# Splitting the last fc2 output group of a DiT block into 192, 128 and 64 columns, with the last two finished by VectorE

## The chip, the cores and the metric

The kernel runs on one core of a Trainium2 chip. Times are device microseconds (us) of one execution; most quotes are medians of several executions. The profile's span of the same execution is about 1.7 to 1.85 us shorter than its time. The engines are named as the profile names them: PE (TensorE matmuls), PEld (its weight loads), DVE (VectorE), ACT (ScalarE), POOL (GpSimd), SP (SyncE, which issues 70 of the 90 DMAs in the trace of the kernel before). A letter q behind an engine means its sequencer.

## The reference, cut to what matters

```python
B, N, D = (2, 256, 1152);  F = 4 * D
...                                        # adaLN, attention, projection give x, h2, gate_m
m = _gelu(h2 @ w_fc1) @ w_fc2              # fc1: [512, 4608], fc2: [512, 1152]
return x + gate_m * m
```

Only the last two lines are touched. In the kernel, fc2 writes 512 rows (4 tiles of 128) by 1152 columns (3 panels of 384); every output group sums over KF = 36 blocks of 128.

## The kernel before

```python
P = 128; PW = 384; KF = 36; NPD = 3; NT = 4
...
    groups = []
    for n in range(NPD):
        for t in range(NT):
            if n == NPD - 1 and t == NT - 1:
                groups.append((n, t, n * PW, 2 * P))                  # 256 columns
                groups.append((n, t, n * PW + 2 * P, PW - 2 * P))     # 128 columns
            else:
                groups.append((n, t, n * PW, PW))
    for gi, (n, t, c0, cw) in enumerate(groups):
        b = t // TPB
        last = gi == len(groups) - 1
        pacc = acc_tile([P, cw], "pacc")
        for kk in range(KF):
            j, r = divmod(n * KF + kk, 27)
            nc.tensor.matmul(pacc[:], gT[:, kk, t * P:(t + 1) * P],
                w_f2[j][:, r, c0 - n * PW:c0 - n * PW + cw],
                start=(kk == 0), stop=(kk == KF - 1))
        tmp = work.tile([P, cw], FP32, name="tmp", tag="tmp", bufs=3)
        nc.vector.tensor_tensor(tmp[:], pacc[:], gate_m[:, b, c0:c0 + cw], op=ALU.mult)
        o_sb = work.tile([P, cw], BF16, name="o_sb", tag="o_sb", bufs=3)
        (nc.vector if last else nc.gpsimd).tensor_tensor(
            o_sb[:], tmp[:], x1[:, t, c0:c0 + cw], op=ALU.add)
        nc.sync.dma_start(out_v[:, b, t % TPB, c0:c0 + cw], o_sb[:])
```

Each group ends in a VectorE multiply out of PSUM, an add (GpSimd, but VectorE for the last group), and an output DMA from SyncE.

## Time and profile before

| quantity | before |
|---|---|
| time, median of the first 3 executions | 242.99 us (242.89 to 243.03) |
| span of the profiled execution | 241.3 us |
| PE busy | 98% of the span |
| start of fc2 (first matmul of L806) to the end | 73.55 us |
| end of the last matmul to the end | 3.10 us |

The last two rows are read from the records of the trace. From the page of the kernel before, here are the busy times of the engines (part 1) and the shares of the chain that ended last (part 4).

```profile
PE 236.3 (98%) x1698; PEld 144.6 (60%) x1698; DVE 91.6 (38%) x194; ACT 60.1 (25%) x122; POOL 28.3 (12%) x47
...
PE 95%; DMA 2%; DVE 1%; SPq 0%; issue 0%; DVEq 0%
```

The kernel is bound by PE. So there are two ways to make it shorter: fewer PE nanoseconds, or a shorter tail behind the last matmul. The next fence is the chain of the kernel before, in order of time, in the window from 224 us on; columns are start in us, length in us, and what it was.

```profile
223.94 14.24 PE pacc L806 x123
238.18 0.03 issue
238.21 0.02 DVEq L812
238.23 0.04 issue
238.27 0.30 DVE tmp L812
238.57 0.02 issue
238.60 0.29 DVE o_sb L814
```

After PE come 0.3 us of multiply and 0.3 us of add on 128 columns; then the output DMA. The costs of the pieces stand in the groups by form, window from 165 us on (line, engine, operation, shapes, count; busy us and mean ns of one; idle time before).

```profile
L806 PE MATMUL pacc<-w_f,gT 128*128 128x384 bf16 x396 | 64.5, 326 | 0.0
L806 PE MATMUL pacc<-w_f,gT 128*128 128x256 bf16 x36 | 4.1, 273 | 0.0
L806 PE MATMUL pacc<-w_f,gT 128*128 128x128 bf16 x36 | 2.2, 219 | 0.0
...
L812 DVE TENSOR_TENSOR tmp<-pacc,gate 128x256 f32<-128x256 f32 x1 | 0.4, 425 | 3.4 <-PE pacc L806 3.4
L812 DVE TENSOR_TENSOR tmp<-pacc,gate 128x128 f32<-128x128 f32 x1 | 0.3, 291 | 1.6 <-PE pacc L806 1.6
L814 DVE TENSOR_TENSOR o_sb<-tmp,x 128x128 bf16<-128x128 f32 x1 | 0.3, 291 | 0.0
```

A matmul's mean ns (326 at 384 columns) is its latency, not its spacing: they overlap. The spacing (start to start, in the trace) is 162.5 ns at 384 columns, 109.2 at 256 and 55.8 at 128. That 2-column matmuls with a new 128x128 weight each can follow one another much faster shows in the timeline of PE at 22 us (start us, length us, engine, line, what, count): nine in 0.37 us, of which 0.163 us is one latency, so some 26 ns each (start to start the records have 28 ns once and 25 seven times).

```profile
22.21 0.37 PE L250 MATMUL pm<-sT,w_scale_a 128*128 128x2 bf16 x9
```

Here are the waits of SyncE in the window 236 to 242 us of the kernel before (who waited for whom: us in total, times, longest), and then, from the instructions of the line that carries the end of the program (L856), SyncE's semaphore checks that fall between the moment the last DMA is seen and the next instruction of SyncE's program end, a drain at 240.44 (window 240.36 to 240.42 us).

```profile
...
SPq L817 <- DVE o_sb L814: 1.0, 1, 1.0
...
SPq L856 <- DMA out_dram<-o_sb: 0.6, 1, 0.6
```

```profile
L856 SPq EVENT_SEMAPHORE  x1: 28/28/28, 240.4 to 240.4; - x1
```

SyncE waited 0.6 us for the last output DMA, and after it had come there was one check record left: the one that waited.

### The profile page before, as it was taken

What the parts mean: (1) busy time and instruction counts of PE and PEld (TensorE: products, weight loads), DVE (VectorE), ACT (ScalarE), POOL (GpSimd) and SP (SyncE); (2) the same over time, 40 slices, a digit from 0 to 9 for tenths busy, and PEclk for the clock granted to TensorE, in tenths of its full rate; (3) what the DMA queues carried; (4) which work ended last, traced back from release to release, by engine and by line L of the source; (5) the groups of instructions that cost most, each with busy time, mean ns of one, the idle gap of its engine ahead of it and who ended that gap; (6) DMA issues with size and microseconds to landing.
All of it is one profiled execution on the core that took longest, in us unless ns stands there. A gap on an engine that the chain in (4) does not pass through costs nothing.

```text
span 241.3 us, 3993 instructions
## 1 busy us (share of the span) xinstructions
PE 236.3 (98%) x1698; PEld 144.6 (60%) x1698; DVE 91.6 (38%) x194; ACT 60.1 (25%) x122; POOL 28.3 (12%) x47
## 2 busy tenths in 40 slices
PE   8899999999999999999999999999999999999994
PEld 5675444466667566888844444444666656666674
DVE  4842442319325678930002999950000000000001
ACT  6732322307215032770423333222000000000000
POOL 2300000001400324100000000001121111111111
PEclk9999999999999999999999999999999999999999
DMA  6999999998599994739999999999300000000000
GB/s 196 324 317 311 376 367 391 389 393 249 99 315 397 387 311 81 196 62 364 390 392 392 339 326 284 285 326 275 98 16 16 20 16 16 19 18 18 26 25 16
DMA packets 48925, 53.30 MB, mean 221 GB/s; under 512 B 9731, under 2 KB 36619, under 8 KB 48907
## 3 DMA queue, kind: packets, MB, share of 16 engines
q1 hardware_dynamic: 41312, 50.14, 62.6%
q10 hardware_dynamic: 7083, 1.72, 4.9%
q0 software_dynamic: 512, 1.19, 2.2%
q8 instruction: 13, 0.21, 0.4%
q14 instruction: 5, 0.04, 0.1%
HBM read 50.15 MB, written 1.19 MB: 213 GB/s over the span
## 4 chain that ended last, share of the span: by engine, by line
PE 95%; DMA 2%; DVE 1%; SPq 0%; issue 0%; DVEq 0%
PE pacc L806 29%; PE pacc L750 29%; PE pacc L697 7%; PE pacc L603 7%; PE pq L525 7%; PE pk L282 5%; PE pk L311 2%; DMA x_sb<-in_x_dram 2%; PE pa L644 2%; PE ps_s L560 2%; PE pn L420 2%; PE pt L267 1%; PE pm L250 1%; DVE stats L195 1%; PE pg L502 0%; SPq L88 0%
## 5 line engine op out<-in xcount | busy, mean ns | idle before, releaser
L750 PE MATMUL pacc<-hT,w_f 128*128 128x256 bf16 (+1 forms) x432 | 70.5, 326 | 0.0
L806 PE MATMUL pacc<-w_f,gT 128*128 128x384 bf16 (+2 forms) x468 | 70.5, 314 | 0.0
L806 PEld LDWEIGHTS <-gT 128*128 128x128 bf16 x468 | 44.4, 98 | 26.2
L750 PEld LDWEIGHTS <-w_f 128*128 128x128 bf16 x432 | 42.2, 98 | 27.6
L812 DVE TENSOR_TENSOR tmp<-pacc,gate 128x384 f32<-128x384 f32 (+2 forms) x13 | 6.9, 527 | 65.6 <-PE pacc L806 57.3
L782 ACT ACTIVATE gT<-pacc 128x512 bf16<-128x512 f32 x24 | 14.3, 597 | 32.7 <-PE pacc L750 32.7
L473 DVE SCALAR_TENSOR_TENSOR part<-w_gate_m,s,part 128x1152 f32<-128x1152 bf16 x16 | 21.4, 1414 | 0.0
L814 POOL TENSOR_TENSOR o_sb<-tmp,x 128x384 bf16<-128x384 f32 (+1 forms) x12 | 11.6, 971 | 53.9 <-DVE tmp L812 53.9
L697 PE MATMUL pacc<-w_o,big 128*128 128x384 bf16 x108 | 17.9, 326 | 0.0
L525 PE MATMUL pq<-hT,w_q 128*128 128x512 bf16 x81 | 17.8, 379 | 0.0
L603 PE MATMUL pacc<-w_v,hT 128*128 128x384 bf16 x108 | 17.7, 326 | 0.0
L603 PEld LDWEIGHTS <-hT 128*128 128x128 bf16 x108 | 10.5, 98 | 7.1 <-issue 0.3
L697 PEld LDWEIGHTS <-big 128*128 128x128 bf16 x108 | 10.4, 98 | 7.2 <-issue 0.4
L525 PEld LDWEIGHTS <-w_q 128*128 128x128 bf16 x81 | 7.9, 98 | 9.4
L282 PE MATMUL pk<-big,w_k 128*128 128x256 bf16 (+1 forms) x72 | 13.2, 325 | 0.0
L703 POOL TENSOR_TENSOR x<-tmp,x_sb 128x384 f32<-128x384 f32 x8 | 7.3, 911 | 26.3 <-DVE tmp L702 26.3
L471 DVE TENSOR_SCALAR part<-w_gate_m,s 128x1152 f32<-128x1152 bf16 x2 | 1.6, 818 | 22.2 <-DMA w_gate_m<-in_w_mod_dram 22.2
L495 POOL DMA_DIRECT2D gates_dram<-nat_v x2 | 1.1, 534 | 67.7 <-DVE nat_v L493 67.7
L282 PEld LDWEIGHTS <-w_k 128*128 128x128 bf16 x72 | 6.8, 97 | 3.5 <-issue 0.2
L771 ACT ACTIVATE gT<-pacc 128x512 bf16<-128x512 f32 x12 | 6.5, 597 | 9.1 <-PE pacc L750 9.1
L516 POOL DMA_DIRECT2D gates_dram<-nat x4 | 2.4, 596 | 49.8 <-DVE nat L513 48.4
L175 PE MATMUL pwarm<-zeros 128*128 128x256 f32 x18 | 6.7, 540 | 1.2 <-DVE eps_t L95 1.2
(106 smaller groups left out, 164.4 us busy)
## 6 DMA issues: line engine op xcount, KB each, us to landing
w_f<-in_w_fc_dram SPq DMA_DIRECT2D x12, 864.0 KB, 14.2
w_f<-in_w_fc_dram SPq DMA_DIRECT2D x3, 1728.0 KB, 10.1
w_f<-in_w_fc_dram SPq DMA_DIRECT2D x2, 2592.0 KB, 17.2
w_gate_a<-in_w_mod_dram SPq DMA_DIRECT2D x3, 864.0 KB, 14.4
w_v<-in_wqkv_dram SPq DMA_DIRECT2D x3, 864.0 KB, 15.4
w_o<-in_wo_dram SPq DMA_DIRECT2D x3, 864.0 KB, 14.7
w_shift_m<-in_w_mod_dram SPq DMA_DIRECT2D x3, 864.0 KB, 9.5
w_scale_m<-in_w_mod_dram SPq DMA_DIRECT2D x3, 864.0 KB, 15.8
```

Source lines behind the costliest of these rows:

```text
L175: nc.tensor.matmul(dst[:, 0:T // 2], zeros32[:, 0:P], zeros32, start=True, stop=True)
L282: nc.tensor.matmul(pk[m][:, c0:c1], w_k[:, k, m * P:(m + 1) * P], hT0[:, k, c0:c1], start=(k == 0 and c0 == 0), stop=(k == KD - 1), skip_g ...
L473: nc.vector.scalar_tensor_tensor(part[:, b, :], wg[:, k, :], s32[:, k, b:b + 1], part[:, b, :], op0=ALU.mult, op1=ALU.add,)
L525: nc.tensor.matmul(pq[m][:], w_q[:, k, m * P:(m + 1) * P], hT[:, k, :], start=(k == 0), stop=(k == KD - 1), skip_group_check=True,)
L603: nc.tensor.matmul(pacc[:], hT[:, k, t * P:(t + 1) * P], w_v[:, k, pnl * PW:(pnl + 1) * PW], start=(k == 0), stop=(k == KD - 1),)
L697: nc.tensor.matmul(pacc[:], aT[:, k, t * P:(t + 1) * P], w_o[:, k, c0:c1], start=(k == 0), stop=(k == KD - 1),)
L703: (nc.gpsimd if pool_add else nc.vector).tensor_tensor(x1[:, t, c0:c1], tmp[:], x_sb[:, t, c0:c1], op=ALU.add)
L750: nc.tensor.matmul(dst, w_f1[m // KD][:, k, ml * P:(ml + 1) * P], hT[:, k, c0:c1], start=start, stop=(k == KD - 1), **kw,)
L782: nc.scalar.activation(gT[:, m, :], pacc[:], ACT.Gelu_apprx_tanh)
L806: nc.tensor.matmul(pacc[:], gT[:, kk, t * P:(t + 1) * P], w_f2[j][:, r, c0 - n * PW:c0 - n * PW + cw], start=(kk == 0), stop=(kk == KF - 1),)
L812: nc.vector.tensor_tensor(tmp[:], pacc[:], gate_m[:, b, c0:c0 + cw], op=ALU.mult)
L814: (nc.vector if last else nc.gpsimd).tensor_tensor(o_sb[:], tmp[:], x1[:, t, c0:c0 + cw], op=ALU.add)
```

## The change

The intent is a shorter tail: only 64 columns instead of 128 are left to multiply, add and store after the last matmul. To keep GpSimd's slower add out of the way (on 128 columns it took 0.45 us in run e7 below, against 0.29 on VectorE), the second to last piece is finished by VectorE too.

```diff
             if n == NPD - 1 and t == NT - 1:
-                groups.append((n, t, n * PW, 2 * P))
-                groups.append((n, t, n * PW + 2 * P, PW - 2 * P))
+                for c0, c1 in ((0, PW // 2), (PW // 2, PW - 64), (PW - 64, PW)):
+                    groups.append((n, t, n * PW + c0, c1 - c0))
...
-        last = gi == len(groups) - 1
+        last = gi >= len(groups) - 2
```

## The prediction

> What bounds the kernel now. The page gives PE 98% busy at a granted clock of 1.0 throughout, and the chain that ended last is 95% PE. The last stage (fc2, 468 matmuls, 29% of the span) is PE back to back: the table of groups shows no PE idle. The chain of waits ends with PE until 238.18 us, VectorE multiply 238.27 (0.29 us), VectorE add 238.60 (0.29), the last output DMA issued at 238.91 (0.33 to issue, landing about 1.1 us after its issue began), then about 1.2 us of program end; span 241.3. So two things matter: the PE time of the last 384 columns, and the 3.1 us tail behind the last matmul.
>
> What the change does. Two accumulation groups (256, 128 columns) become three (192, 128, 64): 36 more weight loads and matmuls, same columns. The new last group leaves 64 instead of 128 columns to finish; the 128-column group is finished by VectorE too and is now second to last. Nothing else moves; one more output DMA on SyncE's queue.
>
> PE cost. In the trace the spacing of matmuls in fc2 is 162.5 ns at 384 columns, 109.2 at 256, 55.8 at 128: a line of 2.5 ns plus 0.417 ns per column. Whether 64 columns follow that line depends on the weight load, which has less to hide under. Each LDWEIGHTS record lasts 98 ns, but they overlap: the 2-column matmuls of the scale section, each with its own 128x128 weights, run at 25 ns spacing in this trace. [...] So I estimate 29.2 ns at 64 columns and 82.5 at 192. PE for the 384 columns: before 36 x (109.2 + 55.8) = 5.94 us; after 36 x (82.5 + 55.8 + 29.2) = 6.03 us. Cost: +0.09 us, all on the chain.
>
> Tail gain. VectorE multiplies took 0.558, 0.425, 0.291 us at 384, 256, 128 columns, 1.05 ns per column, so 0.224 at 64; the add (0.291 at 128) should shrink alike. Two of them: -0.13 us. The last DMA writes 128-byte instead of 256-byte pieces; its packets took 28 ns at 512 bytes, 18 at 256, about 8 per engine: at most -0.04 us; the fixed part stays. Total tail: -0.13 to -0.18.
>
> No new wait: the 128-column group needs about 0.65 us of VectorE after its last matmul while the 64-column group runs about 1.05 us on PE, so VectorE is free in time by about 0.4 us; its output is issued before the last one. Buffers are free microseconds earlier.
>
> Net: +0.09 - 0.13 - 0.03 = about -0.07 us. Predicted 242.9 us, range 242.6 to 243.3; faster by over 2%: 0.005, within 2%: 0.985, slower: 0.01.
>
> What would show it: spacing of the 64-column matmuls near 29 ns (wrong if near 56: PE +1.0 us and time about 243.9); PE's end at about 238.27; last two VectorE records near 0.22 us; last DMA landing about 1.05 us after its issue; chain unchanged in kind.
>
> What would make it wrong: weight loads of real fc2 tiles not keeping up at 64 columns, or PE instructions not being fetched fast enough; VectorE still busy with the 128-column piece when the last one is ready; two small output DMAs close together delaying each other.

A passage of it that compared the spacing of matmuls with figures which no trace of this case shows is cut. No term of the sum goes with it: 29.2 and 82.5 ns come from the line through the three spacings of the trace, and the sum stays +0.09 - 0.13 - 0.03 = about -0.07 us.

## More of the kernel before

Before the program ends, SyncE checks that the DMAs have been confirmed: in the trace of this kernel its last check, that of the last output DMA, starts at 240.38 us, and the program is over 0.89 us later. The framework generates that code, and it is not in this source.

## The result, and the profile after

The changed kernel took 244.02 us (median of 6 executions, 243.40 to 244.44) against 243.01 us (6 executions, 242.89 to 243.35). The ratio of the two is 1.0039 (95% interval 1.0022 to 1.0055): inside 2%, but slower, and outside the predicted range. Ratios in this document are the mean time of one kernel's executions over that of the other's of the same rounds, so they are not quite the ratio of the quoted medians, nor of the plain means of all executions.

The chain of the changed kernel, same view and window start as before:

```profile
223.95 14.33 PE pacc L806 x159
238.28 0.03 issue
238.31 0.02 DVEq L812
238.33 0.04 issue
238.38 0.24 DVE tmp L812
238.61 0.02 issue
238.64 0.23 DVE o_sb L814
```

PE ends 0.10 us later, the two VectorE steps are 0.06 us shorter each. Everything up to here is as predicted. The new groups by form:

```profile
L806 PE MATMUL pacc<-w_f,gT 128*128 128x192 bf16 x36 | 3.1, 246 | 0.0
L806 PE MATMUL pacc<-w_f,gT 128*128 128x128 bf16 x36 | 2.2, 219 | 0.0
L806 PE MATMUL pacc<-w_f,gT 128*128 128x64 bf16 x36 | 1.2, 193 | 0.0
...
L812 DVE TENSOR_TENSOR tmp<-pacc,gate 128x64 f32<-128x64 f32 x1 | 0.2, 225 | 0.4 <-PE pacc L806 0.4
L814 DVE TENSOR_TENSOR o_sb<-tmp,x 128x64 bf16<-128x64 f32 x1 | 0.2, 225 | 0.0
```

The spacing of the 64-column matmuls is 29.1 ns (29.2 estimated), that of the 192-column ones 82.5 (82.5 estimated). VectorE sat idle 0.4 us before the last multiply, so it was free in time. The 64-column multiply and add took 225 ns each (224 estimated).

The difference is at the very end. SyncE's waits of the changed kernel in the same window, and its checks of L856 from the moment at which the last DMA was seen (window 240.30 to 240.80):

```profile
...
SPq L817 <- DVE o_sb L814: 1.7, 2, 1.2
SPq L856 <- DMA out_dram<-o_sb: 0.9, 1, 0.9
...
```

```profile
L856 SPq EVENT_SEMAPHORE  x8: 28/28/28, 240.3 to 240.7; - x8
```

Before, one check record was left when the last DMA had come. Now eight are left: the one that waited and seven more. The starts of these records after the last issue, read from the trace (us; a bar marks the wait for the last DMA; a shorter record just before them is left out):

```
before: 239.35 239.41 239.47 239.53 239.59 239.65 239.71 239.78 | 240.38
after:  239.32 | 240.31 240.38 240.44 240.50 240.56 240.62 240.68 240.74
```

One check takes 0.061 us (0.43 us for seven). The kernel before spends eight of its nine before the last DMA has landed, where they cost nothing; the changed kernel meets the DMA that it must wait for at the second, and does the other seven after it. From the start of the last check to the end of the program, both traces take 0.89 us. Adding up, from the records of the two traces (landing is here the end of the DMA's last packet; its semaphore is complete 0.35 us later, and SyncE's check starts 0.02 us after that):

| step | before | after | difference | predicted |
|---|---|---|---|---|
| start of fc2 to end of the last matmul | 70.45 | 70.54 | +0.09 | +0.09 |
| to the issue of the last DMA | 0.75 | 0.62 | -0.13 | -0.13 |
| issue to landing | 1.10 | 1.06 | -0.04 | -0.03 to -0.04 |
| landing to SyncE seeing it | 0.36 | 0.37 | 0 | 0 |
| seen to end of the program | 0.89 | 1.31 | +0.43 | 0 |
| sum (from unrounded times) | 73.55 | 73.90 | +0.35 | about -0.07 |

This leaves two questions. Is it really the position of the last DMA in the order of checks, or something that the split itself brings? And why did the six executions lose 0.94 us on average (mean 243.99 against 243.05) when the traces differ by 0.35?

Why the position changed was read in the compiled program. In it, the DMAs issued by SyncE and ScalarE (80 in the trace of the kernel before, 81 in that of the changed one) signal eight semaphores in rotation, and a DMA waits for an earlier one of its own number; in the traces 11 of the 13 and 12 of the 14 output DMAs follow a check of the very semaphore that they signal. The last issues are (the compiled program's list, with the waits of each):

```
before  L817 DMACopy out_dram<-o_sb 128x128 [waits DMAHW7_49,DVE_49]
after   L817 DMACopy out_dram<-o_sb 128x64 [waits DMAHW0_49,DVE_49]
```

With 13 output DMAs the last one has number 7, the one checked last; the fourteenth turns the rotation on to number 0, the first of the eight to be checked. That the number in the wait is the DMA's own was an inference when the experiments were planned; they test it, because it predicts exact counts of checks. The kept traces also show it directly, since their records carry the semaphores: the DMAs of SyncE and ScalarE signal 100, 102, 103, 105, 106, 107, 108, 109 in turn (numbers 0 to 7 of this document), and the checks at the end wait for them in this order. The last DMA signals 109 before the change and 100 after it, and each time the record just before it waits for that same semaphore.

### The profile page after: what moved, and what is told of

Its sections match the earlier page's. It is cut to its first block, busy times and chain, and to the rows that moved or that the text cites. A ratio compares the mean times of both kernels' runs of the same rounds, so it can differ in the third digit from the quotient of the medians. Undisturbed runs are those within 1.5% of the kernel's fastest.

```text
span 241.6 us, 4072 instructions
## 1 busy us (share of the span) xinstructions
PE 236.3 (98%) x1734; PEld 145.0 (60%) x1734; DVE 91.9 (38%) x196; ACT 60.1 (25%) x122; POOL 28.2 (12%) x47
## 4 chain that ended last, share of the span: by engine, by line
PE 95%; DVE 2%; DMA 1%; issue 0%; SPq 0%; DVEq 0%
PE pacc L806 29%; PE pacc L750 29%; PE pacc L697 7%; PE pacc L603 7%; PE pq L525 7%; PE pk L282 5%; PE pk L311 2%; PE pa L644 2%; PE ps_s L560 2%; PE pn L420 2%; DMA x_sb<-in_x_dram 1%; DVE stats L195 1%; PE pt L267 1%; PE pm L250 1%; PE pg L502 0%; DVE xn L235 0%
## 5 line engine op out<-in xcount | busy, mean ns | idle before, releaser
L806 PE MATMUL pacc<-w_f,gT 128*128 128x384 bf16 (+3 forms) x504 | 70.5, 303 | 0.0
L806 PEld LDWEIGHTS <-gT 128*128 128x128 bf16 x504 | 44.9, 98 | 25.8
L812 DVE TENSOR_TENSOR tmp<-pacc,gate 128x384 f32<-128x384 f32 (+3 forms) x14 | 7.0, 501 | 65.2 <-PE pacc L806 57.1
L702 DVE TENSOR_TENSOR tmp<-pacc,gate 128x384 f32<-128x384 f32 x12 | 6.6, 549 | 3.1 <-PE pacc L697 3.1
```

The lines of the kernel that those rows point to most:

```text
L702: nc.vector.tensor_tensor(tmp[:], pacc[:], gate_a[:, b, c0:c1], op=ALU.mult)
L806: nc.tensor.matmul(pacc[:], gT[:, kk, t * P:(t + 1) * P], w_f2[j][:, r, c0 - n * PW:c0 - n * PW + cw], start=(kk == 0), stop=(kk == KF - 1),)
```

## The experiments

The theory: the loss is the position of the last DMA in the order of checks (the lane theory). Rivals: the smaller writes or the two small DMAs close together land late; the extra DMA costs as such; the 64-column group disturbs PE; the changed kernel disturbs its own start. All kernels gave correct results. A fine measure is the time from the start of fc2 to the end in the trace; it repeated within 0.01 us for the same kernel.

| run | what | number of the last DMA | checks after it | fc2 to end | median us | ratio to before (95%) |
|---|---|---|---|---|---|---|
| blind | changed kernel | 0 | 7 | 73.90 | 244.02 | 1.0039 (1.0022 to 1.0055) |
| e1 | changed kernel | 0 | 7 | 73.91 | 243.47 | 1.0009 (0.9994 to 1.0024) |
| e2 | before, 1 tiny load | 0 | 7 | 73.97 | 243.68 | 1.0035 (1.0006 to 1.0064) |
| e3 | before, 4 tiny loads | 3 | 4 | 73.81 | 243.57 | 1.0016 (1.0000 to 1.0032) |
| e4 | changed, 7 tiny loads | 7 | 0 | 73.48 | 243.09 | 0.9994 (0.9981 to 1.0006) |
| e5 | changed kernel | 0 | 7 | 73.90 | 243.88 | 1.0030 (1.0012 to 1.0048) |
| e6 | changed, one load fewer | 7 | 0 | 73.48 | 243.28 | 1.0006 (0.9992 to 1.0021) |
| e7 | changed, 128 piece added by GpSimd | 0 | 7 | 73.91 | 243.54 | 1.0022 (1.0004 to 1.0040) |
| e8 | 320 and 64 columns | 7 | 0 | 73.40 | 243.38 | 1.0011 (0.9998 to 1.0024) |
| e9 | before against itself | 7 | 0 | 73.56 | 243.62 | 1.0007 (0.9991 to 1.0022) |
| e10 | changed kernel | 0 | 7 | 73.91 | 243.86 | 1.0030 (1.0010 to 1.0049) |
| e11 | before, 8 tiny loads | 7 | 0 | 73.55 | 243.09 | 0.9992 (0.9978 to 1.0006) |
| e12 | 320 and 64 columns again | 7 | 0 | 73.39 | 243.27 | 0.9997 (0.9977 to 1.0016) |
| e13 to e16 | changed kernel | 0 | 7 | 73.90 to 73.91 | 243.23 to 243.46 | none (one execution each; the kernel before, once beside them: 243.23) |

### Turning the rotation without touching the split (e2, e3, e11)

A tiny load issued after the third output of fc2, when the DMA engines are nearly idle (busy share 0.08 in fc2 of the kernel before), only turns the rotation. n is 1, 4 or 8.

```diff
         nc.sync.dma_start(out_v[:, b, t % TPB, c0:c0 + cw], o_sb[:])
+        if gi == 2:
+            for _ in range(n):
+                nc.sync.dma_start(touch_x[:], x_v[:, 1, 0, 0:32])
```

> The kernel before, with one tiny extra load (8 KB, SyncE's queue) issued after the third fc2 output, which only shifts which of the eight DMA semaphores each later DMA signals: the last one goes from the last-checked to the first-checked. Lane theory: 243.0 + 7 x 0.061 = about 243.4 us, and seven checks of about 0.06 us after the landing in the trace. Rivals (64-column matmuls, 128-byte pieces, close DMAs): unchanged, 243.0.

> The same with four tiny loads: the last DMA signals the fourth semaphore checked. Lane theory: four checks after it, +0.24 us, about 243.25. Rivals: 243.0.

> The kernel before with eight tiny extra loads after the third fc2 output: a full turn of the eight semaphores, so the last DMA is again on the last-checked one. Lane theory: fc2 to end 73.55, as before, although it has more extra loads than the versions with one and four that lost 0.42 and 0.26. Rival, extra DMAs as such cost: 73.9 or more.

The kernel before, with its PE, VectorE and output DMAs unchanged, lost 0.42 us of tail with one load (73.97 against 73.55), 0.26 with four, and nothing with eight. SyncE's checks from the moment at which the last DMA was seen, one fence per kernel (1, 4 and 8 loads):

```profile
L859 SPq EVENT_SEMAPHORE  x8: 28/28/28, 240.3 to 240.7; - x8
```

```profile
L859 SPq EVENT_SEMAPHORE  x5: 28/28/28, 240.8 to 241.1; - x5
```

```profile
L859 SPq EVENT_SEMAPHORE  x1: 28/28/28, 240.2 to 240.2; - x1
```

Each count includes the check that waited, so 7, 4 and 0 follow it, as the rotation says. The split, small writes and a 64-column group are not needed for the loss, and extra DMAs as such cost nothing (73.55 with eight). The timed means of e2 and e3 agree in direction (their medians lie 0.42 and 0.31 us above the 243.26 of the kernel before); one execution of e2 took 245.96 us at a mean granted clock of 0.992, which none of these theories speaks of.

### Turning the rotation back under the split (e4, e6)

e4 is the changed kernel with n = 7 in the same edit. e6 gets there by loading less often, not more:

```diff
-    w_o = load_rows("w_o", wo_v, 0)                       # three loads of 3 row blocks
+    w_o = wide_tile("w_o")
+    for r0, r1 in ((0, 5), (5, KD)):                      # two loads
+        nc.sync.dma_start(w_o[:, r0:r1, :], wo_v[:, r0:r1, 0:D])
```

> The changed kernel with seven tiny loads after the third fc2 output, so that its last DMA again signals the last-checked semaphore. Lane theory: the loss goes and the predicted gain appears, 242.9 to 243.0 us. Rivals in the split itself: still 243.4 to 244.4.

> The changed kernel with the projection weights loaded in two pieces instead of three (they land some 15 us before they are used), so one load fewer in the whole program and the last output DMA again on the last-checked semaphore, without any added transfer. Lane theory: fc2 to end 73.48 us, no check after the last landing, times 0.05 to 0.1 us below the kernel before. Rival, the seven tiny loads of the earlier experiment helped in another way: fc2 to end stays 73.9.

Both gave 73.48 us from fc2 to the end, the number expected for e6, and 0.08 below the kernel before: the gain that the prediction had worked out (0.07). The checks of e6 from the moment the last DMA was seen:

```profile
L858 SPq EVENT_SEMAPHORE  x1: 28/28/28, 240.6 to 240.6; - x1
```

The timed ratios (0.9994 and 1.0006) cannot resolve 0.08 us; that gain is shown by the traces only. The times expected for e6, 0.05 to 0.1 us below the kernel before, did not come: its median was 0.02 below, its mean 0.13 above.

### The change without its second half (e7)

```diff
-        last = gi >= len(groups) - 2
+        last = gi == len(groups) - 1
```

> The changed kernel with the 128-column piece's add given back to GpSimd, so only the last piece is finished by VectorE alone. That piece has about 1 us of the 64-column group to hide under, and GpSimd needs about 0.5 us for it: no change, fc2 to end 73.90 us with seven checks after the landing. If the second half of the change mattered, the last issue would come later than 0.62 us after PE's end.

The timeline of e7 (start us, length us, engine, line, what, idle before):

```profile
238.70 0.45 POOL L814 TENSOR_TENSOR o_sb<-tmp,x 128x128 bf16<-128x128 f32 x1 [1.36 <-DVE tmp L812]
239.38 0.23 DVE L812 TENSOR_TENSOR tmp<-pacc,gate 128x64 f32<-128x64 f32 x1 [0.76 <-PE pacc L806]
239.64 0.23 DVE L814 TENSOR_TENSOR o_sb<-tmp,x 128x64 bf16<-128x64 f32 x1
```

GpSimd's add of the 128 columns is over at 239.15, 0.23 us before VectorE's last multiply begins. The last issue comes 0.62 us after PE's end, as in the changed kernel, and fc2 to end is 73.91. So having VectorE finish the 128-column piece is worth nothing here.

### Two pieces instead of three (e8, e12)

```diff
-                for c0, c1 in ((0, PW // 2), (PW // 2, PW - 64), (PW - 64, PW)):
+                for c0, c1 in ((0, PW - 64), (PW - 64, PW)):
```

> Two pieces of 320 and 64 columns, both finished by VectorE: no extra matmuls (36 x (135.8 + 29.2) = 5.94 us, as before), no extra output DMA, so the last one stays on the last-checked semaphore, and the short tail is kept. Lane theory plus the costs of the prediction: fc2 to PE's end 70.43, issue 0.62 later, landing 1.06, seen 0.37, end 0.89: 73.37 us from fc2 to end, 0.18 below before. Risk: VectorE needs about 1 us for the 320 columns, which the 64-column group just covers; if not, or if its output DMA delays the last one, fc2 to end 73.5 or more.

> The 320 and 64 split again: fc2 to end 73.40 us in the trace, as in its first run. Its times should average 0.15 us below the null copy, which the start-up scatter may hide.

fc2 to end was 73.40 and 73.39 us (expected 73.37), 0.16 to 0.17 below the kernel before, with no added matmul and no added DMA. Groups by form of e8:

```profile
L806 PE MATMUL pacc<-w_f,gT 128*128 128x320 bf16 x36 | 5.1, 299 | 0.0
...
L812 DVE TENSOR_TENSOR tmp<-pacc,gate 128x320 f32<-128x320 f32 x1 | 0.5, 491 | 4.3 <-PE pacc L806 4.3
L812 DVE TENSOR_TENSOR tmp<-pacc,gate 128x64 f32<-128x64 f32 x1 | 0.2, 224 | 0.0
```

VectorE's 0.98 us for the 320 columns just fits under the 64-column group: it shows 0.0 idle before the last multiply, and the last issue still comes 0.62 us after PE's end, as in the changed kernel. In the trace this is the best tail of all. In timed executions it is not shown to be faster: 1.0011 and 0.9997, both intervals holding 1. Its fastest execution, 242.64 us, is also the fastest, but one minimum proves little.

### Where the rest of the 0.94 us went (e1, e5, e9, e10, e13 to e16)

The changed kernel ran unaltered three more times in rounds, once beside a copy of the kernel before (e9), and four times as single looks.

> The changed kernel unaltered, to see whether its times repeat and scatter again. Lane theory (the last output DMA of the changed kernel lands on the semaphore that the end of the program checks first of eight, so seven checks of about 0.06 us each, which before lay under the landing, now follow it): about +0.4 us against the kernel before, in every run. Rival, small writes or two close DMAs: the landing of the last DMA itself varies and is late by 0.4 to 1 us. The measured times so far (243.4 to 244.4) are wider than the lane theory explains by itself, so I expect 243.4 to 244.4 again.

> The changed kernel unaltered, a third sample. Two parts of its loss are to be told apart: the seven late checks (fixed, in the trace from the start of fc2 to the end, 73.90 us against 73.55 before) and a start-up that varied from one execution to the next (0.66 us late by the 150th matmul in the profiled execution of the second sample). Lane theory: mean of its runs about +0.35 us over the mean of the runs of the kernel before, with scatter in both; fc2 to end 73.90. Rival, the changed kernel disturbs its own start-up as well: +0.6 us or more again, with the kernel before quiet.

> The kernel before against itself. All profiled executions so far are alike from the start of fc1 on, apart from the last 3 us; only the first 20 us vary. The start-up scatter theory says that this variation belongs to no kernel: the null shows single executions up to about 1 us above the fastest too, a mean within 0.2 us of the other copy. The rival, that the extra loss of the changed kernel (0.3 us on average beyond its 0.35 us tail, over 18 executions) is its own: the null stays at 0.0 and within 242.8 to 243.6 us. fc2 to end 73.55 either way.

> The changed kernel, beside the null. Both theories: fc2 to end 73.90 in the trace. Scatter theory: mean of its executions minus mean of the null copy about 0.35 us. Rival: 0.6 us or more.

> One look at the changed kernel, to catch one of its executions above 244.2 us in a profile. Start-up theory: fc2 to end 73.90 us whatever the time, and the time follows the start of fc1 (97.0 us in the quick ones, 98 and later in the slow ones). Rival, the tail itself is sometimes longer (last landing or checks): fc2 to end above 74.2 us in a slow one.

> The same, a second look: fc2 to end 73.90 by the start-up theory, above 74.2 in a slow execution by the rival.

> The same, a third look: fc2 to end 73.90 by the start-up theory, above 74.2 in a slow execution by the rival.

> The same, a fourth look: fc2 to end 73.90 by the start-up theory, above 74.2 in a slow execution by the rival.

In every trace, fc1 takes 70.56 us from its first matmul to that of fc2, and the tail of a kernel is constant. Only the start of fc1 moves, from 96.96 to 98.17 us, and the shift has arisen by 26 us: in e7, the latest, L311's first matmul is already 1.02 us later than in the kernel before, and the first matmul of fc1 is 1.02 us later too. These are PE's waits in the first 24 us of e1 (244.06 us), whose fc1 starts at 97.82; the changed kernel's first profiled execution (243.40 us, fc1 at 97.17) waited 0.8 us for xn and had no wait for w_scale_a in this view.

```profile
PE pt L267 <- DVE xn L235: 1.4, 1, 1.4
...
PE pm L250 <- DMA w_scale_a<-in_w_mod_dram: 0.5, 1, 0.5
```

So the start of a kernel scatters by up to 1.2 us in profiled executions, and not only with the split: the two profiled executions of the kernel before (the first and e9) start fc1 at 97.15 and 97.74. What sets it off was not tested; in e1 a late first load is part of it: VectorE waited 0.19 us for x_sb and started its first statistics at 4.64 us, against 4.42 in the kernel before, and PE waited 0.5 us for w_scale_a. The slowest profiled execution (e7, 244.44 us, the changed kernel but for the add) has its fc1 at 98.17 and its tail at 73.91: slow by its start, not by its tail. The copy of the kernel before ranged from 242.91 to 243.94, wider than the 0.14 us of its first three executions had led me to think, and the expectation of at most 0.2 us between the means of two copies held (0.13).

The averages do not close completely. Differences of the plain means of all executions, changed minus before, were 0.94, 0.35, 0.71 and 0.55 us, 0.64 on average, where the traces show 0.35. By the expectations, e5 (0.71) fell on the side of the rival, that the change loses more than its tail; against the null copy e9, e10 lost 0.42, nearer to the 0.35 of the scatter theory. The excess does not follow the split clearly: e4 and e6, which have the split, differ from what their traces show by -0.04 and +0.21 us, and e2, which does not have it, by +0.46 (+0.09 without its slowest execution). The profiled executions, each the first of its run, do not account for the remaining 0.3: fc1 starts at 97.33 us on average in the ten traces with the last DMA on number 0, at 97.34 in the seven with number 7. The four looks (243.23 to 243.46 us, fc2 to end 73.90 or 73.91) did not happen on a slow execution. In the blind rounds and in e10 each second execution of the changed kernel was slower than the one before it by 0.4 to 1.4 us, and those were not profiled. What they lose, and whether it belongs to the change, stays open; no profiled execution of the changed kernel shows a tail longer than 73.91 us.

## Why the prediction was wrong

- That the kernel is bound by PE and that only the PE time of the last 384 columns and the tail matter: right. The windows before fc2 did not change but for scatter (97.15 and 97.17 us up to fc1, 70.56 for fc1 in both).
- PE cost +0.09 us, with 64 columns at 29.2 ns: right (+0.09, 29.1 ns). The weight load, 98 ns for each record, did not bind; this was the main risk named.
- VectorE gain -0.13 us, DMA gain at most -0.04: right (-0.13 and -0.04; a packet of the last output took 18.4 ns at 256 bytes and 12.7 at 128).
- "No new wait": VectorE was free 0.4 us early, as said, and the two small DMAs, issued 0.92 us apart, did not delay each other: the last landed 1.06 us after its issue, against 1.10 before. Still the sentence failed, because it stopped at the last DMA.
- The step that failed is the sum "+0.09 - 0.13 - 0.03". It lacked a term. The prediction had written "about 1.2 us of program end" as a constant and "one more output DMA on SyncE's queue" as free. The runs showed that the program end contains a fixed order of checks of 0.061 us each, and that one more DMA moves the last one from the last to the first of eight: +0.43 us, six times the net gain and of the other sign. e2 shows the term alone (+0.42), e6 shows the sum without it (-0.08).
- The range, 242.6 to 243.3, was too narrow besides. It took the scatter from three executions; the copy of the kernel before, e9, alone spans 1.0 us. With the missing term the forecast would have been about 243.3, at the edge of that range, and the 244.02 of the blind executions would have needed the scatter as well. About 0.3 us of the average loss is not explained by any trace.

## What to carry to other kernels

When a change adds or removes a DMA, look at which semaphore the last DMA of the program gets and where in the final checks it stands: here the last place was best (fc2 to end 73.48 us in e6, against 73.90 with the first), and one load more (e2) or fewer (e6) on SyncE's queue, far from the end, moved it. Read the tail of a trace to its very end, past the last landing; a constant there is a claim to be checked. For gains below the start-up scatter, compare a segment of the trace that repeats (here the start of fc2 to the end, within 0.01 us), and prefer a split that adds neither an instruction nor a DMA (320 and 64 columns, 73.40 us) to one that adds both (73.90).
